# Attention with beacon keys and a soft mixture of experts on one core: V loaded three keys to a partition and sorted by matmuls, q and k loaded four heads at a time, all expert weights given homes, experts with moving weights

## The chip, the cores and the metric

The kernel runs on one of the eight cores of one Trainium2 chip. The metric is the device time of one execution in microseconds (us). A core has a matrix engine (PE, with its weight loads shown apart as PEld), a vector engine (DVE), a scalar engine for activations (ACT), a general engine (POOL), a queue engine that issues transfers (SP), and 16 DMA engines that serve every transfer whoever issues it. Each engine has its own list of instructions and works it off in order; an instruction may wait for semaphores that others set. Matmul results go to PSUM, from where DVE or ACT copy them out.

## The reference

Eight batches of eight heads; 576 queries of 64 numbers a head; 16 extra "beacon" keys stand ahead of the 576 own keys, so there are 592 keys. Beacons are seen by every query, own keys causally. The attention result, 4608 tokens of 512 numbers, goes into a soft mixture of eight experts with four slots each.

```python
scores = q @ concat(beacon_k, k).T / 8          # causal on the own keys only
x = softmax(scores) @ concat(beacon_v, v)       # -> x: 4608 x 512
logits = x @ phi                                # 4608 x 32 slots
d = softmax(logits, over the tokens)
slot_input = d.T @ x                            # 32 x 512, needs all tokens
slot_out[e] = relu(slot_input[e] @ w1[e]) @ w2[e]   # 4 slots an expert, F = 1024
c = softmax(logits, over the slots)
out = c @ slot_out                              # 4608 x 512
```

The slot inputs need every token, so the experts can only start when all attention is done, and the output only when all experts are done.

## The kernel before, in words

The order of each engine's instructions is written out by hand (`manual_schedule`); the framework only adds the semaphores and gives out buffers. The attention loop at the end of the kernel runs over 32 pairs of heads, `n = 0..31`, four pairs (`g = n % 4`) to a batch `b`. One turn of the loop does, in this order:

- `score(n, 0)`: eight matmuls (L202) of 64 rows x 128 columns into PSUM tile `sc0`, then on ACT one exponential (L208) over 128x1024 numbers into `ex`, then on POOL the causal mask (L210).
- one to three queued pieces of routing work for the batch before (`work.pop`), except where `n % 4` is 0.
- `score(n, 1)`: the same with `sc1` (L202, L208, mask L216).
- `transp(n + 1)`: q and k of the next pair are turned by 36 transposes of 64x64 (L187) into two `tr` tiles, and two DVE copies (L189, 128x576) take them out in the right order of tokens; POOL puts the beacon keys in front of k (L192).
- `attend(n - 1, 0)`: 15 matmuls (L229) for the first head of the pair before, into PSUM tile `av0`; DVE takes the reciprocal of the row sums (L236) and multiplies (L237) into `xb`, the tokens of the batch.
- `score(n, 2)` into `sc0`, `attend(n - 1, 1)` into `av1`, `score(n, 3)` into `sc1`.
- transfers and casts for later turns: q and k of pair `n + 5` (`load_pair`, SP, five buffers), one part of V of the next batch (`load_v`, SP, L103, in pieces of 256 bytes, since a key's 64 numbers of one head are all that lies together), a cast of a V part to 16 bits (`cast_v`, L243, on POOL or DVE), and in 20 of the turns one piece of expert weights (`load_w`, POOL's queue, L120, 1 MB read and 512 KB written).

In PSUM `sc0` and `sc1` hold 2 x 512 columns each, `av0` and `av1` 512 each, and the pool `ps_tr`, whose tiles are all called `tr`, has two buffers of 512. Transposes, routing pieces and expert layers take turns in these two. A `tr` tile can be written only when the last reader of the tile that had the buffer is done.

The routing of a batch is seven pieces: three of transposes of `xb` with DVE copies to `xT` (L256, L261, L265), two of logits (L271) with an exponential on ACT (L275), one that turns the exponentials into `dT` (L283, L285), one that adds `dT.T @ xb` to `siacc` (L294, L298).

After the loop come the last routing, the 36 small column sums (L373) and the experts. For an expert, layer 1 takes the weights as the stationary operand: 32 weight loads of 128x128 with matmuls of four columns (L392). ACT applies the relu (L395), and eight matmuls (L397) with `w2` moving, 512 columns and 32 output rows, add to `av0`. 24 of the 32 weight pieces have room before the experts start; the other eight are loaded as experts free their buffers. Then `soh` (L401), and for the output 36 matmuls (L413), read out by ACT (L415) and DVE (L417) in turn, four 128-token blocks to a transfer of 1 MB.

Of the kernel before, what the change touches and what calls it, by code (L numbers as in the profile page):

```python
# [8 lines left out]
FP = mybir.dt.float32  # L9
# [8 lines left out]
def kernel(  # L18
# [24 lines left out]
    NP = B * H // 2  # L43
    NDC = Dm // P
# [3 lines left out]
    assert Dm == H * D and N == B * S and UL == 80 and J == 9  # L48
    ctx.enter_context(tc.manual_schedule())

# [20 lines left out]
    qkp = ctx.enter_context(tc.tile_pool(name="qkp", bufs=5))  # L71
    vfp = ctx.enter_context(tc.tile_pool(name="vfp", bufs=6))
    exq = ctx.enter_context(tc.tile_pool(name="exq", bufs=2))
    sml = ctx.enter_context(tc.tile_pool(name="sml", bufs=4))
    wh = ctx.enter_context(tc.tile_pool(name="wh", bufs=6))
# [5 lines left out]

    qf, kf = {}, {}

    def load_pair(n):
        b, g = divmod(n, H // 2)
        for (d, src, nm) in ((qf, q, "qf"), (kf, k, "kf")):
            t = qkp.tile([P, J, D], FP, name=nm, tag=nm)
            nc.sync.dma_start(
                out=t[:, :, :],
                in_=src[b, 2 * g:2 * g + 2].rearrange("h s d -> (h s) d").rearrange(  # L90
                    "(p j) d -> p j d", j=J))
            d[n] = t

    vf = {}

    def load_v(b, part):
        for c in ((0, 1), (2,), (3,), (4,))[part]:
            vf[(b, c)] = vfp.tile([P, H, D], FP, name="vf", tag="vf")
            if c == 0:
                nc.sync.dma_start(out=vf[(b, c)][0:Nb], in_=beacon_v[b].rearrange("h n d -> n h d"))  # L100
            lo, hi = max(0, c * P - Nb), min(S, (c + 1) * P - Nb)
            p0 = lo + Nb - c * P
            nc.sync.dma_start(out=vf[(b, c)][p0:p0 + hi - lo],  # L103
                              in_=v[b, :, lo:hi, :].rearrange("h p d -> p h d"))

    NPC = 4 * E
    w1h, w2h = {}, {}

    def load_w(m):
        e, r = divmod(m, 4)  # L110
        d, nm = (w1h, "w1h") if r < 2 else (w2h, "w2h")
        if r % 2 == 0:
            d[e] = wh.tile([P, 4096], F16, name=nm, tag=nm)
        o = (r % 2) * 2048
        if r < 2:
            src = moe_w1[e, r * 256:(r + 1) * 256].rearrange("(c p) f -> p c f", p=P)
        else:
            src = moe_w2[e, (r - 2) * 512:(r - 1) * 512].rearrange("(c p) f -> p c f", p=P)
        c = src.shape[1]
        nc.gpsimd.dma_start(  # L120
            out=d[e][:, o:o + 2048].rearrange("p (c f) -> p c f", c=c), in_=src)

    load_pair(0)
    bkf = const.tile([P, B, D], FP, name="bkf")
    nc.sync.dma_start(out=bkf[:, :, :], in_=beacon_k.rearrange("b h n d -> (h n) b d"))
    load_pair(1)
    for part in range(4):
        load_v(0, part)
    phif = const.tile([P, NDC, NSL], FP, name="phif")
    nc.sync.dma_start(out=phif[:, :, :], in_=moe_phi.rearrange("(c p) e -> p c e", p=P))  # L130
    load_pair(2)
    load_pair(3)
    load_pair(4)
# [5 lines left out]
    nc.vector.tensor_copy(out=idh[:, :], in_=idb[:, :])  # L139
    ones = const.tile([P, 1], F16, name="ones")  # L140
    nc.vector.memset(ones[:, :], 1.0)
    qT = [const.tile([P, 5 * P], BF, name=f"qT{i}") for i in range(3)]
    kT = [const.tile([P, 5 * P], BF, name=f"kT{i}") for i in range(3)]
    for i in range(3):
        nc.vector.memset(qT[i][:, 0:Nb], 0.0)
# [4 lines left out]
    eLh = const.tile([NSL, Nb + N], F16, name="eLh")  # L150
    nc.vector.memset(eLh[:, 0:Nb], 0.0)
    dsum9 = const.tile([NSL, 2 * B], FP, name="dsum9")
# [4 lines left out]
    phih = const.tile([P, NDC, NSL], F16, name="phih")  # L157
    bkT = const.tile([P, NP, Nb], BF, name="bkT")
    avs = [ps_av.tile([P, 512], FP, name=f"av{i}") for i in range(2)]
    for a_ in avs:  # L160
        nc.vector.memset(a_[64:P, 4 * DD:5 * DD], 1.0)
# [3 lines left out]
    def beacons():  # L165
# [7 lines left out]
        for r in range(2):  # L173
            nc.vector.tensor_copy(
                out=bkT[64 * r:64 * r + 64, :, :],
                in_=tp[64 * r:64 * r + 64, :, :].rearrange(
                    "p b (g r n) -> p (b g) r n", g=H // 2, r=2)[:, :, r, :])


    def transp(n):  # L180
        for (f, dst) in ((qf, qT[n % 3]), (kf, kT[n % 3])):
            t = f.pop(n)
            tp = ps_tr.tile([P, J, 64], BF, name="tr", tag="tr")
            for j in range(J):
                for po in (0, 64):
                    hi = t[po:po + 64, j, :].bitcast(BF)[:, 1::2]
                    nc.tensor.transpose(tp[po:po + 64, j, :], hi,  # L187
                                        idb[po:po + 64, po:po + 64])
            nc.vector.tensor_copy(  # L189
                out=dst[:, Nb:Nb + S].rearrange("p (s j) -> p s j", j=J),  # L190
                in_=tp[:, :, :].rearrange("p j s -> p s j"))
        nc.gpsimd.tensor_copy(out=kT[n % 3][:, 0:Nb], in_=bkT[:, n, :])  # L192
# [3 lines left out]
    def score(n, st):  # L196
        if st == 0:
            ex[n] = exq.tile([P, 2, EW], F16, name="ex", tag="ex")
        sc = scs[st % 2]
        for (c, kn, u0, un, col) in steps[st]:  # L200
            for a in range(2):
                nc.tensor.matmul(  # L202
                    sc[0:kn, a, col:col + un],
                    kT[n % 3][64 * a:64 * a + 64, P * c:P * c + kn],
                    qT[n % 3][64 * a:64 * a + 64, u0:u0 + un],
                    start=True, stop=True)
# [14 lines left out]
    def attend(n, a):  # L221
        b, g = divmod(n, H // 2)
        h = 2 * g + a
        for i in range(NCH):
            m = P if i < 4 else UL
            for c in range(i + 1):
                kn = P if c < 4 else UL
                o = blk[(c, i)]
                nc.tensor.matmul(  # L229
                    avs[a][0:m, i * DD:(i + 1) * DD],  # L230
                    ex[n][0:kn, a, o:o + m],
                    vh[b % 2][0:kn, c, h, :],
                    start=(c == 0), stop=(c == i))
        r5 = sml.tile([P, NCH], FP, name="r5", tag="r5")
        avv = avs[a][:, 0:NCH * DD].rearrange("p (i d) -> p i d", d=DD)
        nc.vector.reciprocal(out=r5[:, :], in_=avv[:, :, D])  # L236
        nc.vector.tensor_tensor(  # L237
            out=xb[b % 2][:, :, h, :], in0=avv[:, :, 0:D],
            in1=r5[:, :].unsqueeze(2).broadcast_to([P, NCH, D]), op=AL.mult)

    def cast_v(b, c):
        kn = P if c < 4 else UL
        (nc.vector if c % 2 else nc.gpsimd).tensor_copy(out=vh[b % 2][0:kn, c, :, 0:D], in_=vf[(b, c)][0:kn])  # L243


# [3 lines left out]
    def xt_piece(b, cs):  # L249
        if 0 in cs:  # L250
            xT[b] = exq.tile([P, NDC, U], F16, name="xT", tag="xT", bufs=1)
        tp = ps_tr.tile([P, 2, NDC, P], F16, name="tr", tag="tr")
        for ii, i in enumerate(cs):
            m = P if i < 4 else UL
            for t in range(NDC):
                nc.tensor.transpose(  # L256
                    tp[:, ii, t, 0:m],
                    xb[b % 2][0:m, i, 2 * t:2 * t + 2, :].rearrange("p h d -> p (h d)"),
                    idh[0:m, 0:m])
        if len(cs) == 2:  # L260
            nc.vector.tensor_copy(  # L261
                out=xT[b][:, :, P * cs[0]:P * cs[0] + 2 * P].rearrange(
                    "p t (i u) -> p i t u", i=2), in_=tp[:, :, :, :])
        else:
            nc.vector.tensor_copy(out=xT[b][:, :, 4 * P:U], in_=tp[:, 0, :, 0:UL])  # L265
# [45 lines left out]
    wl = 0  # L311
# [141 lines left out]
```

## Time and profile before

Three runs took 240.92, 237.95 and 241.07 us (median 240.92). The profiled execution's own span is 239.4 us.

| stretch of the profiled execution | us |
|---|---|
| start to the first score matmul | 0 to 10.9 |
| 32 turns of the attention loop, to the end of the last exponential | 10.9 to 173.4 |
| last attend, last routing, column sums | 173.4 to 181.5 |
| eight experts | 181.5 to 211.2 |
| `soh` and the output | 211.2 to 239.4 |

| engine | busy us | share of the span |
|---|---|---|
| PE | 187.1 | 78% |
| PEld | 129.1 | 54% |
| DVE | 130.8 | 55% |
| ACT | 127.4 | 53% |
| POOL | 89.4 | 37% |

A busy share is a mean over stages with different limits, so the profile is read by stage. In the timeline a row gives start and duration in us, engine, line, operation, tiles, shape and how many instructions were merged, and in brackets the idle time before it and what ended that. A matmul's duration contains its latency; the time from one start to the next is what it keeps the engine.

### The profile page before, as it was taken

The numbers are of one execution on the slowest core, as the hardware profiler recorded it, in microseconds if no ns is written. First come the engines' busy times: TensorE is split into PE (matmuls) and PEld (weight loads), VectorE is DVE, ScalarE is ACT, GpSimd is POOL, SyncE is SP. The second block draws the span as 40 slices with busy tenths as digits, with TensorE's granted clock in tenths as the row PEclk, the third lists the DMA queues.
The fourth block names the chain that finished last, engine by engine and source line by source line (L and its number), as shares of the span: only waits on it lengthen the run. The fifth ranks groups of instructions, "written<-read, shape, count | busy, mean of one in ns | idle before, by whom it ended". The sixth has DMA issues, their size and how long they took to land.

```text
span 239.4 us, 8048 instructions
## 1 busy us (share of the span) xinstructions
PE 187.1 (78%) x3512; PEld 129.1 (54%) x3512; DVE 130.8 (55%) x304; ACT 127.4 (53%) x187; POOL 89.4 (37%) x161
## 2 busy tenths in 40 slices
PE   0579778869986898797898698899869999979800
PEld 0457566647664766575666476677646445532200
DVE  4583967555777566777667666566652000058800
ACT  2075576747767487776786758477710000057700
POOL 4080645442652732744645363443542420000000
PEclk9999889985999799999999979689996569995555
DMA  6999999999899899999999999272599999919995
GB/s 193 225 300 281 317 225 243 298 258 240 220 248 228 193 230 282 205 273 263 258 317 262 230 201 277 43 127 41 92 161 202 209 206 210 159 81 422 416 413 248
DMA packets 63715, 55.63 MB, mean 232 GB/s; under 512 B 41920, under 2 KB 50112, under 8 KB 62656
## 3 DMA queue, kind: packets, MB, share of 16 engines
q1 hardware_dynamic: 50880, 38.35, 56.3%
q0 software_dynamic: 12800, 16.78, 41.5%
q8 instruction: 27, 0.44, 0.8%
q14 instruction: 8, 0.07, 0.1%
HBM read 62.46 MB, written 9.44 MB: 300 GB/s over the span
## 4 chain that ended last, share of the span: by engine, by line
PE 47%; DMA 16%; ACT 13%; DVE 5%; SPq 5%; POOL 5%; issue 4%; ACTq 0%
DMA vf<-in_v_dram 14%; ACT ex L208 10%; PE av_152 L397 8%; PE sc_156 L202 6%; PE av_152 L229 6%; PE tr L187 6%; PE fp L413 5%; PE tr L256 3%; DVE xT L261 3%; PE tr L392 3%; PE sc_157 L202 3%; SPq L103 3%; PE tr L271 2%; PE av_153 L229 2%; DMA kf<-in_k_dram 2%
## 5 line engine op out<-in xcount | busy, mean ns | idle before, releaser
L208 ACT ACTIVATE ex<-sc_156 128x1024 f16<-128x1024 f32 x64 | 63.0, 984 | 47.4 <-PE sc_156 L202 47.2
L208 ACT ACTIVATE ex<-sc_157 128x992 f16<-128x992 f32 x64 | 48.0, 751 | 12.2 <-PE sc_157 L202 12.1
L210 POOL TENSOR_SCALAR_AFFINE_SELECT ex<-ex 128x1024 f16<-128x1024 f16 x32 | 34.9, 1092 | 46.9 <-ACT ex L208 46.9
L229 PEld LDWEIGHTS <-ex 128*128 128x128 f16 (+2 forms) x960 | 40.6, 113 | 12.8 <-issue 10.9
L397 PE MATMUL av_152<-w2h,hTz 128*32 128x512 f16 x64 | 20.1, 471 | 2.3 <-ACT hTz L395 2.3
L187 PE MATMUL tr<-idb,kf 64*64 64x64 bf16 x576 | 16.6, 204 | 2.0 <-issue 0.8
L261 DVE COPY xT<-tr 128x1024 f16<-128x1024 f16 x16 | 10.5, 687 | 13.2 <-PE tr L256 13.2
L187 PEld LDWEIGHTS <-qf 64*64 64x64 bf16 x576 | 13.4, 118 | 7.4 <-issue 6.2
L187 PE MATMUL tr<-idb,qf 64*64 64x64 bf16 x576 | 16.8, 205 | 0.6 <-DMA qf<-in_q_dram 0.5
L395 ACT ACTIVATE hTz<-tr 128x32 f16<-128x32 f32 x8 | 1.6, 198 | 28.8 <-PE tr L392 28.8
L401 DVE TENSOR_SCALAR soh<-av_152,rd 32x512 f16<-32x512 f32 x1 | 0.7, 737 | 29.0 <-PE av_152 L397 29.0
L187 PEld LDWEIGHTS <-kf 64*64 64x64 bf16 x576 | 14.3, 119 | 2.9 <-issue 2.6
L413 PE MATMUL fp<-soh,eLh 32*128 32x512 f16 x36 | 14.1, 522 | 1.4 <-DVE soh L401 0.8
L415 ACT ACTIVATE osb<-fp,rc 128x512 f32<-128x512 f32 x18 | 11.8, 687 | 5.9 <-PE fp L413 5.6
L202 PE MATMUL sc_156<-qT_129,kT_132 64*128 64x128 bf16 (+1 forms) x110 | 9.6, 276 | 6.9 <-POOL kT_132 L192 4.8
L243 POOL CAST vh_138<-vf 128x512 f16<-128x512 f32 (+1 forms) x12 | 7.7, 639 | 19.0 <-DMA vf<-in_v_dram 19.0
L216 POOL TENSOR_SCALAR_AFFINE_SELECT ex<-ex 80x160 f16<-80x160 f16 x32 | 10.6, 331 | 10.7 <-ACT ex L208 10.3
L202 PEld LDWEIGHTS <-kT_132 64*128 64x128 bf16 (+1 forms) x198 | 8.6, 110 | 11.1 <-POOL kT_132 L192 5.7
L417 DVE TENSOR_SCALAR osb<-fp,rc 128x512 f32<-128x512 f32 x18 | 13.1, 748 | 2.4 <-PE fp L413 1.6
L120 POOL DMA_DIRECT2D w1h<-in_moe_w_dram x16 | 11.5, 724 | 6.6 <-PE tr L392 6.6
L120 POOL DMA_DIRECT2D w2h<-in_moe_w_dram x16 | 12.1, 758 | 4.4 <-PE av_152 L397 4.4
L229 PE MATMUL av_153<-vh_138,ex 128*128 128x65 f16 (+2 forms) x240 | 11.5, 202 | 2.1 <-issue 2.1
(206 smaller groups left out, 318.9 us busy)
## 6 DMA issues: line engine op xcount, KB each, us to landing
qf<-in_q_dram SPq DMA_DIRECT2D x32, 288.0 KB, 6.2
kf<-in_k_dram SPq DMA_DIRECT2D x32, 288.0 KB, 6.3
w1h<-in_moe_w_dram POOLq DMA_DIRECT2D x16, 512.0 KB, 8.6
w2h<-in_moe_w_dram POOLq DMA_DIRECT2D x16, 512.0 KB, 8.9
out_dram<-osb SPq DMA_DIRECT2D x8, 1024.0 KB, 8.2
vf<-in_v_dram SPq DMA_DIRECT2D x24, 256.0 KB, 7.0
vf<-in_v_dram SPq DMA_DIRECT2D x8, 224.0 KB, 6.9
vf<-in_v_dram SPq DMA_DIRECT2D x8, 160.0 KB, 7.2
```

The lines of the kernel that those rows point to most:

```text
L120: nc.gpsimd.dma_start(out=d[e][:, o:o + 2048].rearrange("p (c f) -> p c f", c=c), in_=src)
L187: nc.tensor.transpose(tp[po:po + 64, j, :], hi, idb[po:po + 64, po:po + 64])
L202: nc.tensor.matmul(sc[0:kn, a, col:col + un], kT[n % 3][64 * a:64 * a + 64, P * c:P * c + kn], qT[n % 3][64 * a:64 * a + 64, u0:u0 + un], ...
L208: nc.scalar.activation(ex[n][:, :, o:o + w], sc[:, :, 0:w], AF.Exp, scale=scale)
L210: nc.gpsimd.affine_select(out=ex[n][:, :, 0:512].rearrange("p a (c t) -> p a c t", c=4), in_=ex[n][:, :, 0:512].rearrange("p a (c t) -> p ...
L216: nc.gpsimd.affine_select(out=ex[n][0:UL, :, o:o + UL], in_=ex[n][0:UL, :, o:o + UL], compare_op=AL.is_ge, fill=0.0, base=0, pattern=[[0, ...
L229: nc.tensor.matmul(avs[a][0:m, i * DD:(i + 1) * DD], ex[n][0:kn, a, o:o + m], vh[b % 2][0:kn, c, h, :], start=(c == 0), stop=(c == i))
L261: nc.vector.tensor_copy(out=xT[b][:, :, P * cs[0]:P * cs[0] + 2 * P].rearrange("p t (i u) -> p i t u", i=2), in_=tp[:, :, :, :])
L397: nc.tensor.matmul(sop[0:NSL, :], hTz[:, e, t, :], w2h[e][:, t * Dm:(t + 1) * Dm], start=(e == 0 and t == 0), stop=(e == E - 1 and t == NF ...
L413: nc.tensor.matmul(fp_[:, :], etok(cg, j), soh[:, :], start=True, stop=True)
L415: nc.scalar.activation(osb[:, j, :], fp_[:, :], AF.Copy, scale=rc[:, i:i + 1])
L417: nc.vector.tensor_scalar(out=osb[:, j, :], in0=fp_[:, :], scalar1=rc[:, i:i + 1], scalar2=None, op0=AL.mult)
```

## The change

- **q and k by quads.** `load_quad` brings four heads at once (three buffers). The partition now holds nine tokens of two heads, so a transpose takes all 128 rows: 64 stationary columns, 128 moving. A quad's 36 transposes are split in four groups of 8 or 10 (`transp(m, which, grp)`), one group after `score(n, 1)` and one after `normal(n - 1)`, two turns to a quad. Each group has a `tr` tile and a DVE copy of 512 or 640 numbers.
- **V three keys a partition.** `load_v` brings V of a batch in pieces of 768 bytes (`vst`), two casts (on POOL but for one at the start) make `vsh`, and `spread_v` puts the keys in order with matmuls by 0/1 selector columns, 19 a batch, 512 columns each, into one or two `tr` tiles a turn (ph 0: 7 matmuls into `ta` and `tb`; ph 1: 3 into `ta`, 6 into `tb`; ph 2: 3 into one tile); ACT copies the first tile of a turn to `vh`, DVE the second.
- **attend and normal.** Both heads' 30 matmuls stand together after `score(n, 2)`; one reciprocal and two multiplications follow for both heads (`normal`).
- **Routing** has a fixed place in the turns; `xT` is made in four pieces of 592 columns; the logits have 128 output rows (the 32 slots four times).
- **Weights.** `wh` has 22 buffers of one piece; the last ten pieces go into buffers that `vst`, `vsh` and the quads no longer need. All 32 are issued inside the loop.
- **Experts.** Layer 1 has the slot inputs as the stationary operand (32 columns) and `w1` moving, 8 matmuls of 512 columns at four column positions; ACT and DVE copy the sums out, 8 small matmuls with `sel` add the four positions and turn the result, and layer 2's eight matmuls also write to four column positions of `av`. The output matmul adds those up.
- **Output** in 18 transfers of 512 KB.

```diff
-    def load_pair(n):
...
+    def load_quad(m):
+        b, hq = divmod(m, 2)
         for (d, src, nm) in ((qf, q, "qf"), (kf, k, "kf")):
-            t = qkp.tile([P, J, D], FP, name=nm, tag=nm)
+            t = qkp.tile([P, 2, J * D], FP, name=nm, tag=nm)
             nc.sync.dma_start(
                 out=t[:, :, :],
-                in_=src[b, 2 * g:2 * g + 2].rearrange("h s d -> (h s) d").rearrange(
-                    "(p j) d -> p j d", j=J))
-            d[n] = t
-
-    vf = {}
+                in_=src[b, 4 * hq:4 * hq + 4].rearrange("h s d -> (h s) d").rearrange(
+                    "(t p j) d -> p t (j d)", t=2, j=J))
+            d[m] = t
...
+        if part == 0:
+            nc.sync.dma_start(out=vst[:, 0],
+                              in_=v[b, :, 0:P * VJ, :].rearrange("h (p s) d -> p h (s d)", s=VJ))
...
+    def transp(m, which, grp):
+        f, dst = ((qf, qT[m % 2]), (kf, kT[m % 2]))[which]
+        t = f[m]
+        j0, j1 = JG[grp]
+        tp = ps_tr.tile([P, j1 - j0, P], BF, name="tr", tag="tr")
+        for j in range(j0, j1):
+            for h in range(2):
+                hi = t[:, h, j * D:(j + 1) * D].bitcast(BF)[:, 1::2]
+                nc.tensor.transpose(tp[64 * h:64 * h + 64, j - j0, :], hi, idb[:, :])
+        nc.vector.tensor_copy(
+            out=dst[:, :, Nb:U].rearrange("p a (s j) -> p a s j", j=J)[:, :, :, j0:j1],
+            in_=tp[:, :, :].rearrange("p j (a s) -> p a s j", a=2))
...
+    def normal(n):
+        b, g = divmod(n, 4)
+        h = 4 * (g // 2) + g % 2
+        r5 = sml.tile([P, 2, NCH], FP, name="r5", tag="r5")
+        avv = av[:, :, 0:NCH * DD].rearrange("p a (i d) -> p a i d", d=DD)
+        nc.vector.reciprocal(out=r5[:, :, :], in_=avv[:, :, :, D])
+        for hh in range(2):
+            nc.vector.tensor_tensor(
+                out=xb[b % 2][:, :, h + 2 * hh, :], in0=avv[:, hh, :, 0:D],
+                in1=r5[:, hh].unsqueeze(2).broadcast_to([P, NCH, D]), op=AL.mult)
...
+    def spread_v(b, ph):
+        vb = b % 2
+
+        K1 = VJ * 64
+
+        def mm(t, part, lo, off, j, first, end, m=P, k=64):
+            nc.tensor.matmul(t[0:m, :], vsel[lo:lo + k, off - j:off - j + m],
+                             vsh[lo:lo + k, part, :, j * D:(j + 1) * D], start=first, stop=end)
+
+        if ph == 2:
+            t = ps_tr.tile([P, 512], FP, name="tr", tag="tr")
+            for j in range(VJ):
+                mm(t, 1, 64, 2 + P + K1, j, j == 0, j == VJ - 1, UL)
+            tiles = [(4, t)]
...
+        for x, (c, t) in enumerate(tiles):
+            kn = P if c < 4 else UL
+            o = vh[vb][0:kn, c, :, 0:D]
+            i_ = t[0:kn, :].rearrange("p (h d) -> p h d", h=H)
+            if x == 0:
+                nc.scalar.activation(o, i_, AF.Copy)
+            else:
+                nc.vector.tensor_copy(out=o, in_=i_)
...
+    for n in range(NP):
+        b, g = divmod(n, 4)
+        nq = n // 2 + 1
+        work = routing(n)
+        half = len(work) // 2
+        score(n, 0)
+        score(n, 1)
+        if nq < NQ:
+            transp(nq, n % 2, 0)
         if n == 0:
+            cast_v(0, nc.gpsimd)
+            cast_v(1, nc.vector)
+            for r in range(4):
+                nc.vector.tensor_copy(out=phih[:, :, r, :], in_=phif[:, :, :])
+        for w_ in work[:half]:
+            w_()
+        score(n, 2)
         if n >= 1:
             attend(n - 1, 0)
             attend(n - 1, 1)
+            normal(n - 1)
+        if nq < NQ:
+            transp(nq, n % 2, 1)
+        score(n, 3)
+        for w_ in work[half:]:
+            w_()
+        if n == 0:
+            for ph in range(3):
+                spread_v(0, ph)
+        elif n < 4:
+            spread_v(1, n - 1)
+        elif g < 3 and b + 1 < B:
+            spread_v(b + 1, g)
...
+        while wl < want(n):
+            load_w(wl)
+            wl += 1
...
+    def layer1(e):
+        h1 = scs[e % 2]
+        for hf in range(2):
+            for c in range(NDC):
+                nc.tensor.matmul(h1[32 * c:32 * c + 32, hf, :], siT[:, c, :],
+                                 w1c(e, c, hf * 512, 512), start=True, stop=True)
+        t = exq.tile([P, 2, EW], F16, name="h1s", tag="ex")
+        nc.scalar.activation(t[:, 0, 0:512], h1[:, 0, :], AF.Copy)
+        nc.vector.tensor_copy(out=t[:, 1, 0:512], in_=h1[:, 1, :])
+        h1s[e] = t
```

The routing list `work` of a turn is: g = 0 the `siacc` piece (second half); g = 1 two `xT` pieces, one in each half; g = 2 two logit pieces, one in each half; g = 3 the `dT` piece (first half) and two `xT` pieces (second half). The buffers of `ps_tr` that the tiles of a turn get follow from the built program: in g = 0 and g = 1 the first tile of `spread_v` has the buffer of the second transpose group, in g = 3 the last `xT` piece has it, and in g = 2 the tile of `spread_v` has that of the second logit piece.

## The prediction

> **What bounds the kernel now.** I read first the stretches of time, then the list of waits, then the timeline of single turns.
>
> The stretches (start:end in us, length, busy time and instructions of PE, PEld, DVE, ACT and POOL, granted clock, DMA share, GB/s) behind the loop:
>
> ```profile
> 173.40:181.50 8.10, 5.86 (x115) 4.86 (x114) 3.93 (x15) 1.00 (x5) 2.76 (x4) 1.00 0.98 167
> 181.50:211.20 29.70, 27.37 (x321) 13.70 (x321) 0.57 (x2) 1.58 (x8) 5.78 (x8) 0.77 1.06 186
> 211.20:239.40 28.20, 14.08 (x36) 4.25 (x35) 13.87 (x19) 11.83 (x18) 0.00 (x0) 0.58 0.81 335
> ```
>
> The experts are bound by PE (27.4 of 29.7 us busy), the output by its transfers. The loop, 10.9 to 173.4, is two thirds of the time. Its waits:
>
> ```profile
> ACT ex L208 <- PE sc_156 L202: 47.2, 53, 9.5
> ...
> POOL vh_138 L243 <- DMA vf<-in_v_dram: 19.0, 7, 5.8
> ```
>
> ACT waits for scores, POOL's casts wait for V. The timeline from 113.6 shows the turn without routing pieces (start, duration, engine, line; in brackets the idle time and what ended it):
>
> ```profile
> 113.62 0.40 PE L202 MATMUL sc_156<-qT_130,kT_133 64*128 64x128 bf16 x8 [0.24 <-ACT ex L208]
> ...
> 114.14 1.02 ACT L208 ACTIVATE ex<-sc_156 128x1024 f16<-128x1024 f32 x1 [0.16 <-PE sc_156 L202]
> ...
> 114.88 0.76 DVE L189 COPY qT_128<-tr 128x576 bf16<-128x576 bf16 x1 [0.60 <-PE tr L187]
> ...
> 115.06 0.67 PE L229 MATMUL av_152<-vh_137,ex 128*128 128x65 f16 x15
> 115.06 0.99 ACT L208 ACTIVATE ex<-sc_157 128x992 f16<-128x992 f32 x1
> ...
> 115.66 0.37 PE L202 MATMUL sc_156<-qT_130,kT_133 64*128 64x464 bf16 x2
> ...
> 115.96 0.68 PE L229 MATMUL av_153<-vh_137,ex 128*128 128x65 f16 x15
> 116.07 0.94 ACT L208 ACTIVATE ex<-sc_156 128x928 f16<-128x928 f32 x1
> 116.22 0.18 DVE L236 RECIPROCAL r_2761<-av_152 128x5 f32<-128x5 f32 x1
> ...
> 116.44 0.49 DVE L237 TENSOR_TENSOR xb_141<-av_152,r_2761 128x320 f16<-128x320 f32 x1
> ...
> 116.91 0.51 ACT L208 ACTIVATE ex<-sc_157 128x416 f16<-128x416 f32 x1
> ```
>
> The next turn starts at 117.06: 3.44 us, and the four exponentials last 3.46. That turn is bound by ACT; DVE's work on `av` lies beside it, and PE does not wait for DVE. The three turns with routing, from 98.90, take 4.74, 4.76 and 5.22, so a batch without late transfers is 18.2 us. The mean over the loop is 162.5 / 8 = 20.3; the 2.1 us between are V's, 17 us in all.
>
> **The loop after the change.** What matters is what PE must wait for in its order. After `attend` come the second transpose group, `score(n, 3)`, routing, `spread_v`, and the next `score(n + 1, 0)`. With two `tr` buffers, `spread_v`'s first tile (g = 0, 1) and the last `xT` piece (g = 3) take the buffer of the second transpose group, and must wait until DVE has copied it. On DVE that copy stands behind `normal`, which waits for both attends, which wait behind `score(n, 2)`, which waits for the first exponential. This chain crosses every engine, and nothing of the next turn can start beside it. From the start of `score(n, 0)`, by the rows above:
>
> - first exponential starts at 0.52, lasts 1.02: 1.54. `score(n, 2)` at 1.60; it holds PE 0.30 (115.66 to 115.96): 1.90.
> - two attends: the first holds PE 0.60 (115.06 to 115.66), the second needs 0.67 to its end: 3.17.
> - DVE: 0.04 to the reciprocal, 0.22 from its start to the first product, two products of 0.49 with 0.03 between: 4.44.
> - copy of 640 numbers: 0.76 for 576 and 0.23 for 128 (L285) give 0.83, start 0.03 later: 5.30. PE resumes at 5.36.
>
> Behind it PE has, by turn (a 512-column matmul holds PE 0.22: eight of L397 take 1.90):
>
> - g = 0: `tb` takes the buffer of the `siacc` piece, whose addition (0.29) stands behind the copy: 5.68. Then four steps of 0.22, as `ta` and `tb` use different halves of the rows, and single instructions of L202 on the two halves start 3 to 7 ns apart: PE free at 6.55. ACT's copy of `ta` (0.60, between 0.51 for 416 and 0.94 for 928 columns) stands ahead of the next exponential and moves it 0.35: 6.9. One after the other it would be 7.4.
> - g = 1: nine matmuls, no halves to pair: 5.36 + 1.98 = 7.3.
> - g = 2: `spread_v` takes the second logit piece's buffer. ACT has two logit exponentials of 0.57 (0.385 and 0.185) among its four, ending 0.52 + 3.46 + 1.14 and gaps = 5.25; three matmuls, 5.97; with ACT's copy 6.3.
> - g = 3: five transposes, 0.3: 5.7.
>
> A batch is 26.2 us instead of 18.2. PE's transposes do get fewer (18 of 128 columns a turn for 36 of 64, 0.92 us before), but they lie where PE waits anyway: nothing gained if they run at the old pace, nothing lost if they take 1.0.
>
> Sum of the loop. Start: one quad is twice the first bytes, and four copies (0.69, 0.83) replace two: first score at 12.1 instead of 10.9. First turn 8.4 (POOL's cast of 1536 numbers, three times 0.615, behind two masks, then 19 matmuls with copies between). Turns 1 to 3, no routing but `xT` in the last: 6.5, 7.3, 6.7. Batches 1 to 6: 6 x 26.2 = 157.2. Last batch, without `spread_v` and for two turns without transposes: 4.3, 5.3, 4.8, 4.1. Together 12.1 + 28.9 + 157.2 + 18.5 = 216.7, against 173.4.
>
> **What is hidden or goes.** Transfers: the weights alone land at 205 to 209 GB/s (180 to 200 us), so all 16.8 MB take 81 us; q, k and V at the old 282 GB/s (20 to 30 us) take 102. The sum, 183, ends ahead of 216.7 even if 768-byte pieces of V gain nothing, so V's 17 us of waits go, and the eight late weight pieces cost nothing. If turns were short, 183 would be the floor. POOL: masks 1.42 a turn, a cast 1.85, a weight issue 0.74; two casts in the turn g = 3 push the next mask to about 7.4 us after that turn's start, and its reader stands over 5 us later. DVE's first transpose copies end long before `normal`.
>
> **Behind the loop.** Tail, with `xT` half done and the column sums moved behind layer 1: attend 1.3, normal 1.3, `xT` 1.0, logits and exponentials 1.6, `dT` 0.85, `siacc` 1.15: 7.2 instead of 8.1. An expert now: layer 1 and layer 2 each eight matmuls of 512 columns on four column positions. Pairs that differ in rows alone (L202) or in rows and columns (L187) ran together; columns alone are not in the trace. From both sides: two steps a layer (0.44) or eight (1.76). I take two. With 0.49 for the small matmuls (36 of L373 in 1.3), 0.31 for the relu, 0.44 + 0.44 and 0.2 for hand-overs: 1.9; eight, the first layer (0.6) and the column sums (1.3): 17.1 instead of 29.7; at most 19 more. Output 28.2 as before: as many bytes and copies.
>
> End of the execution: 216.7 + 7.2 + 17.1 + 28.2 = 269.2. The clock: the trace has half speed for 24 us of the loop. A turn at half speed gains about 2.2 us (scores 0.4, attends 0.7, spread 1.1), a third; the same 24 us cost 4 to 6, I add 4. The profiled execution stands 1.5 under the median (239.4, 240.92), so the forecast is 274.7, **275 us**, 14% slower.
>
> A rule weighed beside it: PE changes between tile shapes more often, by my count twice more a turn on the chain. The row: attends start 0.125 us after the last 64x64 transpose (114.93 to 115.06), where the pitch inside is 0.03. The Trainium skill, "TensorEngine Tiling (Array Packing)", section Key Properties, says that changing the tiling mode drains the engine; the trace agrees with 0.1, and by it the sum would be some 6 us higher, an estimate.
>
> **Rivals.**
> - *PE's clock falls* (0.12). Half speed followed idle gaps of PE of 1.7 to 2.7 us (at 25.3, 50.3, 75.9, 135.7); 1.45 at 97.4 did nothing. The new turn has one gap of 1.0 to 1.4. If half the loop ran at half speed: 16 x 2.2 = 35 instead of 4, 306 us. The Trainium skill, "TensorE: Matmul & The Clock Gate", Part 1, wants an idle window of about 3.4 us; the gaps above were shorter, so the measurement decides.
> - *The chain does not bind* (0.11), faster: the buffers come free early and ACT sets the turn, 3.46 + 0.29 (logits) + 0.45 (`ta`) = 4.2. The loop would end at 12.1 + 8.4 + 31 x 4.2 = 151 so the end would be 151 + 7.2 + 17.1 + 28.2 + 1.5 = 205 us, or 216 where the transfers last to 183 and the last expert waits for them. For it: V's waits go and DVE is 55% busy. Against: the order of DVE. It decides at a mean turn of 5.5 us (no change); I forecast 6.4.
> - *Columns alone do not run together* (0.07): +19, 294 us.
> - *The forecast* (0.70), between 258 and 292 by itself (`tb` in pairs or not, tile changes, clock).
>
> The range 250 to 300 leaves out the second rival and the far half of the first. This measurement can tell about 2% from no change. Faster 0.11 (the second rival), within 2% 0.04 (the forecast's low edge), slower 0.85.
>
> **What would show it.** Right: turns of 5.5 to 7.5 us; PE idle ahead of `spread_v` and of the last `xT` piece, ended by DVE's transpose copy; hardly a wait for V; the experts in under 20 us. Wrong: turns near 4.4 with ACT always busy, or PE at half speed over long stretches, or experts of 4 us each.

## The result, and the profile after

| | median us (range, runs) |
|---|---|
| before, beside the changed kernel | 240.31 (237.95 to 241.07, 4) |
| changed | 280.13 (276.94 to 282.33, 4) |
| ratio | 1.163, 95% interval 1.151 to 1.175 |

An execution more than 1.5% above the fastest of its kernel counts as slow; medians and ranges in this text are of all executions, ratios to the kernel before of the others alone, and the profiled executions of `before_both`, `warm`, `score_early` and `score_early_warm` were slow ones.

The forecast was 275 us. The profiled execution of the changed kernel has a span of 278.6 us. Its stages, with start and end in us, length, busy time and number of instructions of each engine, granted clock, DMA share and GB/s (the loop, the tail, the experts, the output):

```profile
12.20:220.80 208.60, 169.32 (x2559) 111.54 (x2560) 103.88 (x229) 123.41 (x180) 89.91 (x126) 0.93 0.89 203
220.80:228.20 7.40, 4.98 (x99) 3.85 (x100) 4.18 (x15) 0.99 (x4) 0.00 (x0) 1.00 0.79 130
228.20:250.20 22.00, 18.18 (x228) 6.67 (x229) 6.40 (x14) 5.59 (x16) 0.00 (x0) 0.54 0.01 1
250.20:278.60 28.40, 11.54 (x36) 3.75 (x35) 13.24 (x19) 11.62 (x18) 0.00 (x0) 0.74 0.84 332
```

The loop ends at 220.8 instead of 173.4; all that the change loses is there. The experts take 22.0 instead of 29.7, at about half clock (0.54). PE has 0.81 of its time busy in the loop, so it is not full either.

The waits of the changed kernel (who waits for whom: us in all, times, longest):

```profile
ACT ex L246 <- PE sc L243: 52.5, 40, 10.8
...
ACT vh L323 <- PE tr L291: 41.8, 24, 3.4
...
POOL vsh L282 <- DMA vst<-in_v_dram: 11.7, 1, 11.7
...
PE tr L291 <- DVE kT L223: 7.5, 8, 1.0
...
PE tr L336 <- DVE kT L223: 5.4, 6, 1.0
...
PE tr L291 <- DVE qT L223: 4.9, 7, 1.2
```

V is waited for once, in the first turn. In its place the engines wait for each other: ACT for scores and for `spread_v` (L291), and PE for DVE's transpose copies (L223), 21 times ahead of `spread_v` and of the last `xT` piece (L336), 17.8 us in all. One turn with g = 0 of batch 2, in the chain of work (start, us, what; pieces in order of time, each released by the one before):

```profile
74.12 1.03 ACT ex L246
...
75.19 0.37 PE sc L243 x2
75.57 1.12 PE av L267 x30
...
76.71 0.23 DVE r L275
...
76.97 0.89 DVE xb L277 x2
77.86 0.74 DVE qT L223
...
78.64 0.56 PE tr L291 x2
...
79.53 0.58 PE tr L291 x4
80.12 0.26 ACT vh L323
...
80.60 1.03 ACT ex L246
```

From 74.12 to 80.60 each step starts only when the one before it is done: an exponential, the second score pair, both attends, `normal` (L275, L277), the copy of the second transpose group (L223), and only then `spread_v`, ACT's copy of it and the next exponential. Turns at full clock take 6.48, 7.05, 5.67 and 5.36 us (g = 0 to 3, start to start of the first exponential, batch 2), together 24.6.

### The profile page after: what moved, and what is told of

Read it like the earlier page. It is cut to its first block, busy times and chain, and to the rows that moved or that the text cites. A ratio compares the mean times of both kernels' runs of the same rounds, so it can differ in the third digit from the quotient of the medians.

```text
span 278.6 us, 6843 instructions
## 1 busy us (share of the span) xinstructions
PE 207.7 (75%) x2960; PEld 128.5 (46%) x2960; DVE 135.5 (49%) x293; ACT 142.9 (51%) x219; POOL 95.5 (34%) x139
## 3 DMA queue, kind: packets, MB, share of 16 engines
q0 software_dynamic: 12800, 16.78, 36.9%
## 4 chain that ended last, share of the span: by engine, by line
PE 51%; DVE 19%; ACT 14%; issue 6%; DMA 4%; POOL 1%; DVEq 0%; SPq 0%; ACTq 0%; POOLq 0%
PE av L267 14%; PE tr L291 13%; ACT ex L246 9%; PE sc L243 8%; DVE xb L277 8%; DVE kT L223 4%; DMA qf<-in_q_dram 4%; PE av L492 3%; PE tr L346 3%; PE tr L222 3%; PE sc L476 2%; DVE qT L223 2%; DVE r L275 2%; ACT vh L323 2%; ACT eLh L350 2%
## 5 line engine op out<-in xcount | busy, mean ns | idle before, releaser
L246 ACT ACTIVATE ex<-sc 128x1024 f16<-128x1024 f32 (+3 forms) x128 | 105.4, 871 | 53.1 <-PE sc L243 52.5
L243 PE MATMUL sc<-qT,kT 64*128 64x128 bf16 (+5 forms) x576 | 55.0, 262 | 12.7 <-ACT ex L246 10.1
L291 PE MATMUL tr<-vsh,vsel 64*128 64x512 f16 (+2 forms) x144 | 39.5, 437 | 17.3 <-DVE kT L223 7.5
L267 PE MATMUL av<-vh,ex 128*128 128x65 f16 (+2 forms) x960 | 42.4, 207 | 0.4 <-DVE xb L277 0.4
L243 PEld LDWEIGHTS <-kT 64*128 64x128 bf16 (+1 forms) x576 | 27.6, 101 | 26.9 <-issue 18.1
L223 DVE COPY kT<-tr 128x512 bf16<-128x512 bf16 (+1 forms) x32 | 24.7, 772 | 14.4 <-PE tr L222 14.4
L223 DVE COPY qT<-tr 128x512 bf16<-128x512 bf16 (+1 forms) x32 | 24.7, 772 | 10.7 <-PE tr L222 10.1
L275 DVE RECIPROCAL r<-av 128x10 f32<-128x10 f32 x32 | 7.1, 221 | 46.4 <-PE av L267 46.4
L277 DVE TENSOR_TENSOR xb<-av,r 128x320 f16<-128x320 f32 x64 | 28.4, 486 | 1.1
L282 POOL CAST vsh<-vst 128x1536 f16<-128x1536 f32 x15 | 21.6, 1462 | 13.0 <-DMA vst<-in_v_dram 11.7
L291 PEld LDWEIGHTS <-vsel 64*128 64x128 f16 (+2 forms) x144 | 11.2, 104 | 31.3 <-issue 23.0
L336 PE MATMUL tr<-idh,xb 128*128 128x128 f16 (+1 forms) x160 | 14.4, 224 | 5.9 <-DVE kT L223 5.4
L133 POOL DMA_DIRECT2D w<-in_moe_w_dram x22 | 16.3, 741 | 0.0
L336 PEld LDWEIGHTS <-xb 128*128 128x128 f16 (+1 forms) x160 | 9.9, 101 | 9.2 <-issue 6.6
```

What stands on the lines that cost most here:

```text
L133: nc.gpsimd.dma_start(out=t[:, 0:2048].rearrange("p (c f) -> p c f", c=c), in_=src)
L223: nc.vector.tensor_copy(out=dst[:, :, Nb:U].rearrange("p a (s j) -> p a s j", j=J)[:, :, :, j0:j1], in_=tp[:, :, :].rearrange("p j (a s) - ...
L243: nc.tensor.matmul(sc[0:kn, h, col:col + un], kt[hh, a_, P * c:P * c + kn], qt[hh, a_, u0:u0 + un], start=True, stop=True)
L246: nc.scalar.activation(ex[n][:, :, o:o + w], sc[:, :, 0:w], AF.Exp, scale=scale)
L267: nc.tensor.matmul(av[0:m, hh, i * DD:(i + 1) * DD], ex[n][0:kn, hh, o:o + m], vh[b % 2][0:kn, c, h, :], start=(c == 0), stop=(c == i))
L277: nc.vector.tensor_tensor(out=xb[b % 2][:, :, h + 2 * hh, :], in0=avv[:, hh, :, 0:D], in1=r5[:, hh].unsqueeze(2).broadcast_to([P, NCH, D]) ...
```

## The experiments

Each is compared with runs of the kernel before on the same chip; the medians of these were between 237.4 and 239.8 us, so a difference of 2 us between two experiments on different chips says nothing. Batches are counted from 0, and turns are measured as above. "Loop end" is the end of the last exponential in the profiled execution (173.4 before, 220.8 changed).

### The chain through DVE: two orders

`normal_late`:

```diff
             attend(n - 1, 1)
-            normal(n - 1)
         if nq < NQ:
             transp(nq, n % 2, 1)
...
         for w_ in work[half:]:
             w_()
+        if n >= 1:
+            normal(n - 1)
```

> The changed kernel, but `normal` of the turn before is issued behind the second half of the routing instead of ahead of it, so that DVE's copy of the second transpose group no longer stands behind the reciprocal and the two products (1.1 us of DVE). Theory (the copy behind `normal` is what PE waits for in every turn): in the turns g = 0, 1 and 3 PE resumes about 0.8 us earlier, g = 2 keeps its length; a batch falls from 24.4 to about 22.1 us and the kernel by about 16, to some 264 us. Rival (PE's own added work sets the turn and the wait is only where its slack shows): under 3 us, 277 or more.

Measured: 258.24 us median (256.06 to 260.49; before 237.37). Turns 5.90, 6.41, 5.21, 4.72, a batch of 22.24, as expected (22.1), though g = 2, which should have kept its length, is shorter by 0.46 too; the loop ends at 195.5. The chain in a g = 0 turn:

```profile
69.67 1.11 PE av L267 x30
...
71.23 0.84 DVE qT L223
...
72.11 0.62 PE tr L291 x2
```

`normal` has left the chain; the copy of the second transpose group (L223) is still what lets `spread_v` start. The kernel gained some 22 us where 16 were expected. Of the 25.3 us between the loop ends, 13 are six batches of 24.4 against 22.24, 3.5 the first four turns, 0.6 the last four, and some 8 the slow-clock stretches of the changed kernel's loop (its batches 3 to 6 took 27.36, 27.41, 25.27 and 25.63 instead of 24.4). Those stretches are gone. The clock in 40 slices of the span (each digit is the granted clock in tenths of full speed, 9 for full), the changed kernel:

```profile
PEclk9999999999999975996699799999899995557975
```

and with `normal` late, where the loop fills the slices to the thirtieth:

```profile
PEclk9999999999999999999999999999999975558975
```

`t_early`:

```diff
             transp(nq, n % 2, 0)
+            transp(nq, n % 2, 1)
...
-        if nq < NQ:
-            transp(nq, n % 2, 1)
```

> The changed kernel, but the second transpose group is issued right behind the first, ahead of the second score pair; `normal` keeps its place. Theory: the DVE copy of that group then runs before `normal` and its buffer is free when `spread_v` asks for it, but the routing's second half still waits for DVE work behind `normal`; g = 0, 1 and 3 get shorter by 0.7 to 0.9, g = 2 longer by about 0.3: about 2 us a batch, 14 in all, some 266 us. Rival (PE's own work sets the turn): under 3 us.

Measured: 249.05 us, ratio to before 1.052 (1.047 to 1.057); about 31 less than the changed kernel where 14 were expected. Turns 5.78, 6.61, 5.41, 4.03: a batch of 21.83, so 2.6 shorter instead of 2. g = 3 gained most (1.3); g = 2, expected 0.3 longer, was 0.3 shorter. As above, the clock stayed full in the whole loop, which is 8 of the difference, and the first four turns gave 5.7.

`t_early_normal_late`:

> The changed kernel with both: the second transpose group ahead of the second score pair, and `normal` behind the routing. Theory: nothing of the chain through DVE is left ahead of `spread_v`, the turns are those of the exponentials and of ACT's copy for `spread_v`, about 5.2, 5.7, 5.5 and 4.3 us, a batch of 20.7: about 255 us, at most 263. If even this stays above 270, the chain that the prediction names is not what sets the turn.

Measured: 246.46 us (255 expected), ratio 1.043 (1.037 to 1.049). Turns 5.49, 6.17, 5.41, 4.03, a batch of 21.1 (20.7 expected); the loop ends at 183.9. The chain of its g = 0 turn:

```profile
64.19 1.11 PE av L267 x30
...
65.49 0.61 PE tr L369 x20
...
66.12 0.30 DVE siacc L373
...
66.46 0.37 PE tr L291
```

Neither `normal` nor a transpose copy is in it; PE runs nearly through, and what is left of DVE is `siacc` (0.30). Moving two calls takes 34 of the 39 us of loss back (spans 239.4, 278.6 and 244.2), so the cause that the prediction named is shown. It is not all of one kind: the loop ends 36.9 earlier, and of that 20.8 are shorter turns of the six middle batches, 8 their slow-clock stretches, 7.0 the first four turns and 1.1 the last four. What still stands against the kernel before: the loop ends 10.5 us later. The first exponential is 1.3 later, the first four turns take 29.9 instead of 20.2, which is most of it, six batches 125.7 instead of 123.7, and the last batch 2.6 less; 5.6 come back behind the loop.

### What `spread_v` costs

`no_spread`:

```diff
         elif n < 4:
             spread_v(1, n - 1)
-        elif g < 3 and b + 1 < B:
-            spread_v(b + 1, g)
```

> The changed kernel without `spread_v` from batch 2 on: the values of batches 2 to 7 stay those of batches 0 and 1, while all loads and casts of V are kept. That part of the computation is left out. Theory (the selector matmuls lie at the end of a chain, so that what goes with them is the wait for the transpose copy as well as their 3.4 us of PE a batch): turns of about 4.2, 5.1, 5.0 and 5.4, a batch of 19.7 instead of 24.4, 28 us less: about 252. Rival (only the matmuls' own time on PE goes): 3.4 us a batch, 20 less, about 260.

Measured: 241.24 us, ratio 1.021 (1.014 to 1.027), loop end 181.4. Batches 4 and 5, at full clock, take 4.20, 5.12, 4.20 and 5.38: 18.9. That is 5.5 less than 24.4, more than the 3.4 of PE's own time, so the wait at the chain's end went with the matmuls. The time fell below the expected 252 because the batches were 0.8 shorter than expected, about 5 us in six, and because half speed cost 3.8 us in this loop (batches 2, 3 and 6) instead of 8.

`score_early` tries to get more out of the mended order:

```diff
         score(n, 3)
+        if n + 1 < NP:
+            score(n + 1, 0)
         for w_ in work[half:]:
             w_()
```

(`score(n, 0)` at the turn's start goes, `score(0, 0)` stands ahead of the loop.)

> The kernel with the second transpose group early and `normal` late (246.5 us), and in it the first score pair of the next turn issued right behind the fourth of this one, ahead of the routing's second half and of `spread_v`. Theory (what still sets a turn is that ACT waits for scores which stand behind `spread_v`, while PE has no further work to add): a batch falls from 21.1 us towards PE's own work, 152.8 us busy in the 171.7 us of the loop, so 18.5 to 19.5, and the kernel by 10 to 15, to 232 to 236. Rival (the transfers have become the bound: their engines show a share of 1.01 in that loop): the turns get shorter at first and then wait for V, q, k or the last weight pieces, under 4 us less.

Measured: 253.71 us, ratio 1.057 (1.050 to 1.065), where the kernel it was made from had 1.043: some 3 us slower by the ratios, 7 by the medians. Both expectations missed. Turns 3.93, 6.42, 6.31, 5.02, a batch of 21.7, and after the first turns nobody waits for a transfer; the transfers are not the reason. Its chain from the end of a g = 3 turn into the next:

```profile
111.10 0.84 DVE xT L340 x2
...
112.10 0.90 DVE xb L277 x2
...
113.04 1.16 PE av L267 x30
```

Now the attends wait for `normal` of the turn before, because there is only one `av`. The shortest turn fell under 4 us and the others paid: the wait for DVE moved to another place. The profiled execution took 256.67 us, and the three quickest, 250.76 to 252.25, left no profile; that this wait makes all of the difference is not shown.

### V as it was

`v_direct` is the kernel with both orders mended, but with V's loads and casts of the kernel before, started two turns or more ahead (the weights also get 23 buffers instead of 22, and go out slightly earlier):

```diff
-        elif g < 3 and b + 1 < B:
-            spread_v(b + 1, g)
...
+        if b + 1 < B:
+            for c in ((0, 1, 2), (3,), (4,), ())[g]:
+                load_v(b + 1, c)
+            for c in ((), (), (0, 1), (2,))[g]:
+                cast_v(b + 1, c)
+        if g == 0 and b > 0:
+            for c in (3, 4):
+                cast_v(b, c)
```

> V undone alone: the kernel with the second transpose group early and `normal` late (246.5 us), but V loaded as in the kernel before (one key a partition, pieces of 256 bytes, cast straight into `vh`, no selector matmuls), its loads two or more turns ahead of their casts; q and k by quads, all weight pieces homed and the new experts stay. Theory (with the order mended, what is left of the loss is `spread_v`: 3.4 us of PE a batch and its passes through the two `tr` buffers): a batch of about 18, loop end near 160, 220 to 226 us, faster than both kernels. Rival (V's small pieces keep the queues full, so the waits for V come back and the loop ends at the transfers' floor of 183 us, as now): 240 to 247 us.

Measured: 246.03 us, ratio 1.028 (1.014 to 1.041): within 2% of the time with `spread_v` (246.46, 1.043), and not the 220 to 226 of the theory. One batch met no late transfer and took 3.80, 4.79, 5.09 and 4.21, 17.9 us, as the theory said. The others took up to 27.4. Two lines of its waits:

```profile
POOL vh L271 <- DMA vfx<-in_v_dram: 38.9, 10, 6.1
...
DVE vh L271 <- DMA vfx<-in_v_dram: 8.5, 2, 4.5
```

47 us of waits for V, where the kernel before had 32. One on DVE (start, us, in brackets the idle time before it and its end) held back transposes and routing:

```profile
74.38 1.09 DVE L271 CAST vh<-vfx 128x512 f16<-128x512 f32 x1 [4.53 <-DMA vfx<-in_v_dram]
```

The loop ends at 182.7. So the selector matmuls do what they are for; they take away these waits, at a price of about 3 us a batch (21.1 against 17.9). By the parts of the loop they gain more than they cost: the six middle batches take 134.6 us here and 125.7 with `spread_v`. But the first four turns take 20.0 here and 29.9 with it, 6.4 of that in the first turn, which holds all 19 matmuls for batch 0, and that takes the gain back. That the waits came back, as the rival said, is shown. That the loop ends at the floor of 183 us, which the prediction worked out from bytes and rates, fits; it was not tested apart, and `t_early_normal_late` ends at 183.9 too, where after the first turn no wait for a transfer is longer than 0.2 us.

`before_late_casts`:

```diff
-                for c in ((), (0, 1), (2,), (3, 4))[g]:
+                for c in ((), (), (0, 1), (2,))[g]:
                     cast_v(b + 1, c)
+            if g == 0 and b > 0:
+                for c in (3, 4):
+                    cast_v(b, c)
```

> The kernel before with V's casts moved one turn later (two in g = 2, one in g = 3, two in g = 0 of the batch that uses them), so that each load has a turn more to land. Theory (the 17 us of waits for V come from too little lead): they go, about 225 us. Rival (V's small packets keep the queues full, and a longer lead only moves the wait): 5 us less at most, 235 or more.

Measured: 235.59 us, ratio 0.981 (0.973 to 0.989). The waits for V fall from 32 us to 16, the loop ends 4.4 us earlier. This is the rival's size: a longer lead hides half of them. It also suggests that the waits for V, 17 us of the loop in the prediction, were worth less, since half of them bought 4.4.

### The experts

`before_experts`, the essential lines:

```diff
+                nc.tensor.matmul(h1[32 * c:32 * c + 32, hf, :], siT[:, c, :],
+                                 w1h[e][:, c * F + hf * 512:c * F + hf * 512 + 512],
...
+            nc.tensor.matmul(avs[0][32 * c:32 * c + 32, :], hTz[:, e, f, :],
+                             w2h[e][:, f * Dm:(f + 1) * Dm],
```

> The kernel before with the experts of the change alone: layer 1 with the tokens stationary on four column positions, small matmuls through the selector, layer 2 on four column positions; V, q and k, the 24 weight homes as before, and the last eight pieces loaded as experts 0 and 1 are done. Theory: the experts take about 22 us as in the changed kernel instead of 29.7, unless the last pieces hold them up: 6 to 8 us less, about 233 us. Rival (the late weight pieces, not PE, set the end of the experts): no change.

Measured: 239.33 against 239.39 us, ratio 0.996 (0.991 to 1.001): no change. The rival holds. The first six experts take 2.7 us each, then PE waits for the last pieces:

```profile
194.70 1.04 PE L409 MATMUL av<-w2h,hTz 128*32 128x512 f16 x8 [0.48 <-ACT hTz L406]
198.92 0.61 PE L392 MATMUL sc<-w1h,siT 128*32 128x512 f16 x2 [3.18 <-DMA w1h<-in_moe_w_dram]
```

In the changed kernel, with all 32 pieces home, the same experts took 22.0; the shorter experts and the homes pay together.

`before_both`:

> The kernel before with the new experts and with V's casts one turn later: if both act by themselves the gains add up, 10 to 20 us less than before, 220 to 231 us; if the late weight pieces or the transfers are the next limit, less than 6 us.

Measured: 235.56 us, ratio 0.981 (0.974 to 0.988), the same as with the late casts alone; the new experts add nothing. These two are the only versions here that are faster than both kernels, by about 2%.

`warm`:

```diff
         nc.scalar.activation(hTz[:, e, :, e * SPE:(e + 1) * SPE], hp[:, :, :], AF.Relu)
+        for f in range(2):
+            nc.tensor.matmul(av[:, 1, :], idh[:, :], w2c(e, f), start=True, stop=True)
```

> The changed kernel with two further 512-column matmuls an expert into a buffer that nobody reads, issued behind layer 1 where PE waits for the copies. Theory (the experts run at half clock because PE is too little busy there): the clock stays at full speed, an expert falls from 2.7 to about 2 us, 5 us less in all, 275. Rival (the clock's fall has another cause): the added matmuls cost their own time, 0.4 us an expert, 3 us more.

Measured: 275.41 us (268.51 to 276.68; before 239.39). With one of four executions 7 us quicker than the others, the total says little; the stage says it. The experts, from the first copy of layer 1 to the first output matmul, take 17.6 instead of 22.0 us. One expert of the changed kernel, layer 2 to layer 2, with ACT's two steps between:

```profile
233.99 1.05 PE L492 MATMUL av<-w,hTz 128*32 128x512 f16 x8 [0.48 <-ACT hTz L489]
...
236.68 1.04 PE L492 MATMUL av<-w,hTz 128*32 128x512 f16 x8 [0.48 <-ACT hTz L489]
```

and one with the added matmuls (L491):

```profile
236.46 0.62 PE L494 MATMUL av<-w,hTz 128*32 128x512 f16 x8
...
237.66 0.59 PE L491 MATMUL av<-w,idh 128*128 128x512 f16 x2
...
238.30 0.61 PE L494 MATMUL av<-w,hTz 128*32 128x512 f16 x8
```

2.69 us become 1.84, with more work in them, because the clock is full after the first two experts. The theory holds.

`score_early_warm` adds the same two matmuls to `score_early`, and loads the second quad of q and k ahead of V's first part:

```diff
     load_quad(0)
+    load_quad(1)
     load_v(0, 0)
     load_v(0, 1)
-    load_quad(1)
```

> The same, with the two further matmuls an expert that keep PE busy while it waits for the copies, and with the second quad of q and k loaded ahead of V's first part. Theory: the experts keep more of the full clock, 3 to 6 us less, and the first turn, which waits 3.6 us for that quad, gives 1 to 3 more: 225 to 231. Rival (V's first part then lands later and the first turn waits for it as long as before; the clock falls all the same): no difference to the kernel beside it, or up to 3 us more.

Measured: 248.84 us, ratio 1.045 (1.036 to 1.055): 3 us less than `score_early` by the ratios, 5 by the medians, and far from the 225 to 231 of the theory, which stood on a base that had missed. The experts explain it (22.4 to 17.6 us). The first four turns sum to 32.9 against 32.8: the quad came earlier, V later, as its rival said.

`v_direct_warm`:

> The same with the two further matmuls an expert that keep PE busy. Theory: as there and 4 to 5 us less in the experts, about 217 to 222 us. Rival (with a shorter loop the last weight pieces land while the experts run and set their end): no difference to the kernel beside it.

Measured: 240.13 us, ratio 1.001 (0.995 to 1.007), 6 less than `v_direct` (experts 22.4 to 17.2). That is the theory's gain, on the base that `v_direct` really had; the 217 to 222 stood on a base that had missed.

## Why the prediction was right, and where it was off

The forecast of 275 and its cause held. By its own steps:

- **The chain of a turn.** Counted from `score(n, 0)` (73.60 in the turn shown): first exponential at 0.52, forecast 0.52; attends from 1.90, forecast 1.90; their end 3.07, forecast 3.17. `normal` and the copy end at 4.99 instead of 5.30, a third of it the earlier attends, and most of the rest that the two products took 0.89 together instead of twice 0.49 and a gap. PE resumed at 5.04 (forecast 5.36); the further wait for `siacc`, forecast to last to 5.68, ended at 78.78, beside `spread_v`'s first matmul for `ta`, and was no step of its own. The two orders show the chain to be the cause, since taking it apart gives back 34 of 39 us. In a middle batch it is half of the loss: 24.4 us with the chain, 21.1 without it, and 17.9 without `spread_v` as well.
- **The turns.** Forecast 6.9, 7.3, 6.3, 5.7, a batch of 26.2; measured at full clock 6.48, 7.05, 5.67, 5.36, together 24.6 or less. Too long by 1.6 to 1.8 a batch, 10.7 us over six. Of the prediction's signs, the turns at full clock were there but for g = 3, just under its 5.5, and so were the waits for DVE's copies and the missing waits for V; experts under 20 us were not.
- **The clock's term.** 4 us were added for half speed. The loop's four slow stretches cost some 8, the experts 4 to 5. The working took half speed to follow gaps of 1.7 us and more; its list left out one of the half-speed stretches that it had counted in its 24 us, at 151.12 in the kernel before, which followed no gap of PE over 0.8 us.
- **The first turns.** 28.9 forecast for turns 0 to 3, 36.9 measured: the term that fell shortest. (Loop end: 216.7 forecast, plus 8.0 here, less 10.7 for the shorter turns, plus 8.1 for the clock, less 1.3 for the first score and the last batch together, is 220.8, as measured. Errors of 8 to 11 us cancelled, and that the total came so near is in part luck.) The first turn's 8.4 was worked out from POOL's cast and 19 matmuls at full clock. The transposes stood ahead of them and waited for the second quad, loaded behind V, and then nine matmuls took 3.77 us, 0.42 each and not 0.22, as at half speed (the chain of the first turn in the changed kernel):

```profile
6.74 10.12 DMA qf<-in_q_dram
...
16.90 0.66 PE tr L222 x5
...
23.27 3.77 PE tr L291 x9
```

- **What goes.** V's waits went but for the first, as forecast, and the eight late weight pieces cost nothing. That transfers would not bind held. The matmuls at different column positions ran together: four of L492 start 3 to 4 ns apart (from 236.68 in the changed kernel).
- **Behind the loop.** Tail 7.4 (7.2 forecast), output 28.4 (28.2). Experts 22.0 against 17.1: the steps were right for full clock, as 17.2 to 17.6 with PE kept busy show; what failed is that the working let them run at full clock.
- **The rivals.** PE's clock fell in part, at the size named above, not over half the loop. That the chain does not bind is excluded by the two orders. Columns ran together; their price, had they not, is 21 us by the prediction's own figures (16 layers of 1.32) and not 19. Of the rule weighed beside the sum, changes of tile shape, the trace shows the step and not the 6 us: in the turns shown, steps between matmuls of `spread_v` that change the shape took 0.30 to 0.33 us (at 78.83, 79.14 and 85.54), steps that do not, about 0.22, and the turns came out shorter than even the sum without that rule.

## What to carry to other kernels

In an order written by hand, follow the buffer that the next instruction takes back to its last reader, and that reader's place in its engine's queue; here one DVE call ahead of a copy made four engines take turns. Before paying with matrix work for a transfer that is late, price both in the same order, and price the first turns apart: here 3 us a batch bought off somewhat longer waits, and the start took the gain back. A step that is shortened pays only if what feeds it (the last weight pieces) comes sooner too, and only at the clock that it then gets.

## What the runs showed of the hardware that was not expected

- **The clock falls without a long gap.** In these traces the granted clock changes on a grid of 3.41 us. In the changed kernel's loop, from its first record at 38.9 on, it fell behind stretches of that grid in which PE was busy for 0.52, 0.54, 0.55 and 0.66 of the time, and was kept behind the 41 others that had begun at full clock, the least of them 0.61. No gap in the four was longer than 1.0 us. Three stretches of the changed kernel: one that kept the clock (2.24 of 3.42 us busy, 0.65), one that did not (1.89 of 3.41, 0.55), and the one behind that, at 0.50 (columns as in the stages above; PE's busy time comes first after the length):

```profile
52.55:55.97 3.42, 2.24 (x29) 0.88 (x24) 2.02 (x5) 0.94 (x2) 0.97 (x2) 1.00 1.03 182
...
96.93:100.34 3.41, 1.89 (x38) 1.35 (x38) 2.39 (x5) 1.73 (x3) 3.05 (x4) 1.00 0.68 202
100.34:103.75 3.41, 3.09 (x59) 2.56 (x55) 1.85 (x5) 1.61 (x3) 1.49 (x3) 0.50 1.03 240
```

  With `normal` late the least stretch in the loop had 0.69, and no clock fell; nor did it fall in the loops of `t_early` and `t_early_normal_late`, while in `warm`, whose loop is that of the changed kernel, it fell six times. The order of the calls thus cost twice: the wait, and half speed after it. The Trainium skill, "TensorE: Matmul & The Clock Gate", Part 1, puts the window at about 3.4 us, and the grid agrees; it has the clock fall after an idle window, and here stretches busy for half were enough, so the measurement decides. The share of busy time is not a border, though: 0.66 fell here and 0.61 did not, and in the kernel before a stretch at 0.57 kept the clock and one at 0.73 lost it (both ran at full clock themselves; the stretch behind the second ran at half speed):

```profile
96.50:99.91 3.41, 1.96 (x39) 1.57 (x38) 1.62 (x6) 2.01 (x4) 2.99 (x6) 1.00 1.06 184
147.70:151.12 3.42, 2.51 (x72) 1.79 (x69) 1.96 (x8) 2.68 (x4) 1.16 (x2) 1.00 0.90 161
```

  Nor does it explain the experts: their clock fell behind a stretch at 0.74 (from 226.63) and stayed at half with PE busy for 0.7 to 0.87 of each stretch. That more matrix work keeps their clock is shown; what the chip counts stays open.
- **Matmuls of different work overlap when they use different rows.** In the g = 1 turns, `spread_v` for rows 64 to 127 and the next turn's scores on rows 0 to 63 ran side by side (timeline of the changed kernel, batch 3: start, us):

```profile
113.85 0.38 PE L291 MATMUL tr<-vsh,vsel 64*128 64x512 f16 x1
...
113.86 0.23 PE L243 MATMUL sc<-qT,kT 64*128 64x128 bf16 x1
```

  In batch 2, at full clock, they lie the same way (from 86.29). That may be part of why the turn took 7.05 there and not 7.3; it was not tested.
